# A banded-convolution stage on TensorE in larger products: up to ten tiles per product, one head per PSUM bank, two rounds per unit

## The chip, the cores and the metric

The kernel runs on one core of a Trainium2 chip. The metric is the device time of one execution in microseconds (us). Engines are named PE (TensorE, matrix products), PEld (its weight loads), DVE (VectorE), ACT (ScalarE), POOL (GpSimd, which here issues nearly all input transfers) and SP (which issues most output transfers).

A ratio below is the mean time of one kernel's fast runs over the mean of the other's fast runs of the same rounds, so it is not quite the ratio of the medians that are quoted beside it. Runs over 1.5% above the fastest of the same kernel count as slow and are left out of ratios.

## The reference

The computation has two parts. A depthwise causal convolution with seven softmax-normalized taps per head (8 heads of 24 channels) goes over x of 8 x 3264 x 192. Its output u feeds a spectral mixing: a real FFT along the sequence, the lowest 64 modes multiplied by complex 192 x 192 matrices, an inverse FFT, a residual, and a ReLU branch.

```python
out = np.einsum('hk,bskhg->bshg', w, x_unf)          # seven taps, per head
X = np.fft.rfft(x, axis=1)                           # x is the convolution's output
Yr = einsum('bmd,mde->bme', Xr, w_r) - einsum('bmd,mde->bme', Xi, w_i)
Yi = einsum('bmd,mde->bme', Xr, w_i) + einsum('bmd,mde->bme', Xi, w_r)
y = np.fft.irfft(Y, n=S, axis=1)
u = x + y
return u + np.maximum(u @ w_ch, 0.0)
```

## The kernel before

x lies in SBUF as bf16 tiles of 128 sequence positions: 26 tiles for each of four pairs of batches (104 slots in all).

**The convolution.** Taps are put into 64 x 64 band matrices, and PE runs four 64 x 64 array tiles side by side: lower and upper 64 rows, to lower and upper 64 output partitions. Each PSUM bank receives products from a lower and from an upper row tile. A turn (an empty instruction that waits for the earlier products) separates the two steps, so that another row tile follows on a bank only when the first is done. A unit is 4 or 5 tiles of all eight heads: 32 products, two steps each of 8 per half. ACT and DVE each copy half of the heads out of PSUM.

```python
UNITS = ((0, 5), (5, 5), (10, 4), (14, 4), (18, 4), (22, 4))      # per pair of batches
...
def conv(q, t0, n):
    done = [conv_step(q, t0, n, half, 0) for half in range(2)]
    for half in range(2):
        turn(done[half])
        conv_step(q, t0, n, half, 1)
    ...                                   # half 0 copied out by ScalarE, half 1 by VectorE
```

**What is laid between the convolution's units.** The angle tables (parts 2 and 3 are built after the first two units), the low-frequency transform (`dft_unit`, into a `low` bank), and transposes of finished tiles (`some`, one bank of eight blocks per call).

```python
for k, u in enumerate(units):
    conv(*u)
    if k < 2:
        table(*PARTS[k + 1])
    ...
    if k:
        q, t0, n = units[k - 1]
        dft_unit(q, t0, n)
        ...
            some(XJOBS[k], min(NT * q + t0 + n, NT * (NQ - 1)))
```

**The weights of the mixing.** They come in 16 groups of 0.59 MB (as bf16). There are buffers for eight groups: four in `arena`, four lent by `cc`, the not yet needed transposed x of the last pair. Loads of groups 8 to 11 wait for mixing groups 0 to 3; loads of 12 to 15 wait for groups 8 to 11.

```python
for g in range(NL + NW):                  # NL = 4, NW = 4
    load_w(g)

def mix(g):
    ...                                   # 12 products with wbuf(g)
    if g < NW:
        load_w(g + NW + NL)
    elif g >= NW + NL:
        load_w(g + NW)
```

## Time and profile before

| kernel before | value |
|---|---|
| median of three runs | 181.06 us (180.78 to 181.16) |
| span of the profiled run | 179.3 us |
| input transfers without a pause | about 5 to 105 us |
| convolution on PE (L303) | 10.5 to 71.2 us, 816 products |
| mixing group 0 starts | 74.31 us |
| mixing group 15 starts | 106.82 us |
| output stage | 72.5 us |

Read it in two stages. Up to group 15 the transfers of x (at about 190 GB/s written) and then of the weights (at about 206) fill the time; after it PE fills the output stage. The GB/s row of the page's slices shows a pause in the transfers as a lower number, and the time at which group 0 starts tells how late PE is.

### The profile page before, as it was taken

To read this page: it belongs to the slowest core of one execution; us is meant where nothing else is said; L and a number is where in the kernel's file an instruction comes from. 1 tells how busy PE (TensorE), PEld (TensorE's weight loads), DVE (VectorE), ACT (ScalarE), POOL (GpSimd) and SP (SyncE) were. 2 spreads that over 40 slices of the span, in tenths; PEclk is the share of its full clock that TensorE was granted. 3 is DMA by queue.
4 is the path that set the end of the run, shared out by engine and by line. 5 is a ranking of instruction groups with operands and counts; after the bars stand their busy time and mean duration, and the time that the engine had idled before them with its cause. 6 is when DMAs were issued, how large, how long until landed. Compare 5 with 4: busy or idle time off the path is not lost.

```text
span 179.3 us, 6296 instructions
## 1 busy us (share of the span) xinstructions
PE 147.0 (82%) x2736; PEld 109.0 (61%) x2736; DVE 112.1 (63%) x159; ACT 98.4 (55%) x134; POOL 68.8 (38%) x113
## 2 busy tenths in 40 slices
PE   0047569999999999699677769999999999999940
PEld 0034337666667666477465757888776778888820
DVE  1878555674865675334435443788676878888870
ACT  8176643735553734247445355576775676666630
POOL 7999998878866534335244000000000500000000
PEclk9999979999999999979999999999999999999995
DMA  3999999999999999999999950589987799999993
GB/s 42 170 181 188 190 189 189 190 192 190 192 191 190 205 207 206 206 206 206 206 206 206 207 93 4 173 275 300 366 296 268 227 324 362 364 358 347 356 362 131
DMA packets 62875, 40.17 MB, mean 224 GB/s; under 512 B 28800, under 2 KB 62784, under 8 KB 62848
## 3 DMA queue, kind: packets, MB, share of 16 engines
q0 software_dynamic: 36224, 20.08, 80.5%
q1 hardware_dynamic: 26624, 19.69, 32.7%
q8 instruction: 21, 0.34, 0.8%
q14 instruction: 6, 0.05, 0.1%
HBM read 39.40 MB, written 20.05 MB: 332 GB/s over the span
## 4 chain that ended last, share of the span: by engine, by line
DMA 33%; PE 29%; issue 23%; POOL 7%; DVE 4%; ACT 1%; DVEq 0%; POOLq 0%
DMA arena<-in_moe_w_i_dram 13%; PE z L303 8%; DMA cc<-in_moe_w_i_dram 6%; PE low L329 6%; DMA arena<-in_moe_w_r_dram 5%; DMA out_dram<-arena 5%; POOL xall L145 4%; DMA xall<-in_x_dram 3%; PE za L508 3%; PE zb L508 3%; PE za L488 3%; PE zb L488 2%; PE low L383 2%; DVE xall L323 1%; DVE arena L559 1%
## 5 line engine op out<-in xcount | busy, mean ns | idle before, releaser
L303 PE MATMUL z<-xall,band 64*64 64x192 bf16 (+3 forms) x816 | 27.4, 263 | 16.3 <-ACT band L189 10.5
L145 POOL DMA_DIRECT2D xall<-in_x_dram x48 | 38.5, 814 | 5.2 <-DMA xall<-in_x_dram 2.7
L323 DVE CAST xall<-z 128x768 bf16<-128x768 f32 (+1 forms) x24 | 24.5, 1021 | 14.4 <-PE z L303 13.7
L303 PEld LDWEIGHTS <-band 64*64 64x64 bf16 x816 | 18.3, 110 | 24.5 <-ACT band L189 10.9
L321 ACT CAST xall<-z 128x768 bf16<-128x768 f32 (+1 forms) x24 | 20.4, 850 | 22.1 <-PE z L303 22.1
L488 PEld LDWEIGHTS <-cc 64*128 64x128 bf16 x600 | 27.1, 94 | 6.6 <-issue 1.8
L559 DVE TENSOR_TENSOR arena<-za,xall 128x768 f32<-128x768 f32 x26 | 24.8, 956 | 6.1 <-ACT za L534 2.0
L534 ACT ACTIVATE za<-za 128x768 f32<-128x768 f32 (+1 forms) x27 | 21.0, 783 | 9.5 <-PE za L508 9.2
L559 DVE TENSOR_TENSOR arena<-zb,xall 128x768 f32<-128x768 f32 x23 | 21.9, 956 | 6.3 <-ACT zb L534 2.9
L534 ACT ACTIVATE zb<-zb 128x768 f32<-128x768 f32 (+1 forms) x25 | 19.6, 782 | 10.1 <-PE zb L508 8.6
L329 PE MATMUL low<-xall,ftab 128*128 128x384 bf16 x100 | 21.6, 343 | 0.0
L383 PEld LDWEIGHTS <-xall 128*128 128x128 bf16 x300 | 18.7, 105 | 3.2 <-issue 0.3
L548 POOL DMA_DIRECT2D out_dram<-arena x4 | 2.4, 615 | 42.4 <-DVE arena L540 42.4
L488 PE MATMUL za<-wc,cc 64*128 64x192 bf16 x318 | 17.9, 243 | 0.4 <-DVE arena L559 0.4
L508 PE MATMUL za<-mixa,ftab 64*128 64x384 bf16 (+1 forms) x120 | 18.1, 304 | 0.0
L508 PE MATMUL za<-mixa,fsin 64*128 64x384 bf16 (+1 forms) x120 | 18.1, 304 | 0.0
L358 DVE COPY cc<-r 128x1024 bf16<-128x1024 bf16 (+1 forms) x16 | 10.2, 670 | 12.3 <-ACT xs L444 6.0
L508 PE MATMUL zb<-mixa,ftab 64*128 64x384 bf16 (+1 forms) x100 | 16.1, 313 | 0.4 <-ACT zb L534 0.4
L508 PE MATMUL zb<-mixa,fsin 64*128 64x384 bf16 (+1 forms) x100 | 16.1, 313 | 0.0
L488 PE MATMUL zb<-wc,cc 64*128 64x192 bf16 x282 | 15.9, 243 | 0.0
L356 ACT COPY cc<-r 128x1024 bf16<-128x1024 bf16 (+1 forms) x9 | 8.9, 990 | 10.2 <-PE r L383 8.2
L508 PEld LDWEIGHTS <-ftab 64*128 64x128 bf16 x220 | 11.8, 94 | 3.9 <-issue 1.5
(108 smaller groups left out, 185.2 us busy)
## 6 DMA issues: line engine op xcount, KB each, us to landing
out_dram<-arena SPq DMA_DIRECT2D x45, 384.0 KB, 4.6
xall<-in_x_dram POOLq DMA_DIRECT2D x24, 192.0 KB, 6.9
xall<-in_x_dram POOLq DMA_DIRECT2D x16, 240.0 KB, 6.7
arena<-in_moe_w_r_dram POOLq DMA_DIRECT2D x12, 288.0 KB, 9.5
arena<-in_moe_w_i_dram POOLq DMA_DIRECT2D x12, 288.0 KB, 10.1
out_dram<-arena SPq DMA_DIRECT2D x10, 192.0 KB, 2.5
xall<-in_x_dram POOLq DMA_DIRECT2D x8, 144.0 KB, 6.3
cc<-in_moe_w_r_dram POOLq DMA_DIRECT2D x4, 288.0 KB, 11.8
```

Source lines behind the costliest of these rows:

```text
L145: nc.gpsimd.dma_start(out=xall[:, s0:s0 + nf, i, :], in_=src)
L303: mm = nc.tensor.matmul(ov[c], band[r, h, c.start + shift + 64 * (r is UP and c is LO): c.start + shift + 64 * (r is UP and c is LO) + 64] ...
L321: nc.scalar.copy(out=dst, in_=srcv)
L323: nc.vector.tensor_copy(out=dst, in_=srcv)
L329: nc.tensor.matmul(xp, ftab[:, t, :], xall[:, slot(q, t), :, :], start=(t == 0), stop=False, skip_group_check=True)
L356: nc.scalar.copy(out=out, in_=in_)
L358: nc.vector.tensor_copy(out=out, in_=in_)
L383: nc.tensor.transpose(tp[:, P * k:P * k + P], src, ident[:])
L488: nc.tensor.matmul(zt[:, i, D * k:D * k + D], cc[r, q, 3 * t + j, :], wc[r, j, :], start=(k == 0 and j == 0), stop=False, skip_group_check ...
L508: nc.tensor.matmul(zt[:, i, D * k:D * (k + w)], tabs[c][r, t, :], zw[r, q:q + w, c, which, :], start=False, stop=end and k + w == len(duo) ...
L534: nc.scalar.activation(out=zt[:, :, 0:w], in_=zt[:, :, 0:w], func=ACT.Relu)
L559: nc.vector.tensor_tensor(out=o[:, :, :].rearrange("p k (i d) -> p i k d", i=2), in0=zt[:, :, 0:2 * D].rearrange("p i (k d) -> p i k d", k=2),
```

## The change

The intent is fewer and longer products. A unit is up to ten tiles and is done in two rounds of four heads; one head fills one bank, so a product has up to 480 columns instead of 240. The last two units stay at four tiles. Convolution products fall from 816 to 496.

```diff
+    cunits = [(q, t0, n) for q in range(NQ) for t0, n in (((0, 5), (5, 5), (10, 8), (18, 8)) if q == 0 else
+                                                         ((0, 10), (10, 8), (18, 8)) if q < NQ - 1 else
+                                                         ((0, 10), (10, 8), (18, 4), (22, 4)))]
...
-    def conv_step(q, t0, n, half, step):
+    def conv_step(q, t0, n, hp, step):
...
-                o = cp[:, jj, 0:2 * GRP * n].rearrange("p (t i e) -> p t i e", t=n, i=2)
+            o = Z[hp % 2][:, j, 0:2 * GRP * n].rearrange("p (t i e) -> p t i e", t=n, i=2)
...
-    def conv(q, t0, n):
-        done = [conv_step(q, t0, n, half, 0) for half in range(2)]
-        for half in range(2):
-            turn(done[half])
-            conv_step(q, t0, n, half, 1)
+    def conv(q, t0, n, part):
+
+        hps = (2 * part, 2 * part + 1)
+        done = [conv_step(q, t0, n, hp, 0) for hp in hps]
+        for hp, names in zip(hps, done):
+            turn(names)
+            conv_step(q, t0, n, hp, 1)
...
-    for k, u in enumerate(units):
-        conv(*u)
-        if k < 2:
-            table(*PARTS[k + 1])
...
+    for k, u in enumerate(cunits):
+        for part in range(2):
+            conv(*u, part)
+            if part and k < 2:
+                table(*PARTS[k + 1])
...
+                n0 = (n + 1) // 2
+                dft_unit(q, t0 + n0 * part, n - n0 if part else n0)
...
+                    some(part or k % 3 == 0, min(NT * q + t0 + n, NT * (NQ - 1)))
```

More of the change, by code (lines that the diff above doesn't have):

```diff
@@ L266 @@
     LO, UP = slice(0, 64), slice(64, P)
-    def conv_step(q, t0, n, half, step):
-        cp = Z[half][:, :, :].rearrange("p k (j c) -> p (k j) c", j=2)
+    def conv_step(q, t0, n, hp, step):
         s0 = slot(q, t0)
@@ L274, in conv_step @@
         last = t0 + n == NT
-        end = step == 1
         res = []
-        for j in range(2):
-            for own in (True, False):
-                jj = 2 * ((step if own else 1 - step)) + j
-                h = 4 * half + jj
-                dsl = slice(GRP * h, GRP * h + GRP)
-                o = cp[:, jj, 0:2 * GRP * n].rearrange("p (t i e) -> p t i e", t=n, i=2)
-                first = step == 0 and j == 0
-                cur, prev = xall[:, s0 + 1:s0 + 1 + n, :, dsl], xall[:, s0 + k0:s0 + n, :, dsl]
-                if own:
-                    ms = [(LO, LO, o, cur, 0), (UP, UP, o, cur, 0)]
-                    if last:
-                        ms.append((UP, UP, o[:, n - 1, 0, :], xall[:, s0 + n - 1, 1 - q // 2, dsl], 64))
-                else:
-                    m, k1 = (n - 1 if last else n), (n - 1 if last and q >= 2 else n)
-                    ms = [(LO, UP, o[:, 0:m, :, :], cur[:, 0:m, :, :], 0),
-                          (UP, LO, o[:, k0:k1, :, :], prev[:, 0:k1 - k0, :, :], 64)]
-                    if k1 < n:
-                        ms.append((UP, LO, o[:, n - 1, 0, :], xall[:, s0 + n - 1, 1, dsl], 64))
-                res.append([(r, c, ov, mv, h, shift, first) for r, c, ov, mv, shift in ms])
@@ L297, in conv_step @@
-        names = []
-        for pair in (res[0:2], res[2:4]):
-            for k in range(3):
-                for lst in pair:
-                    if k < len(lst):
-                        r, c, ov, mv, h, shift, first = lst[k]
-                        mm = nc.tensor.matmul(ov[c], band[r, h, c.start + shift + 64 * (r is UP and c is LO):
-                                                          c.start + shift + 64 * (r is UP and c is LO) + 64],
-                                              mv[r], start=first and k < 2, stop=end, skip_group_check=True,
-                                              tile_position=(r.start, c.start))
-                        names.append(mm.ins.name)
@@ L308, in conv_step @@
-        return names[-6:]
-    def conv(q, t0, n):
-        done = [conv_step(q, t0, n, half, 0) for half in range(2)]
-        for half in range(2):
-            turn(done[half])
-            conv_step(q, t0, n, half, 1)
-        s0 = slot(q, t0)
-        for half in range(2):
-            cp = Z[half][:, :, :].rearrange("p k (j c) -> p (k j) c", j=2)
-            dst = xall[:, s0:s0 + n, :, 96 * half:96 * half + 96].rearrange("p t i (j e) -> p j (t i) e", j=4)
-            srcv = cp[:, :, 0:2 * GRP * n].rearrange("p j (c e) -> p j c e", e=GRP)
-            if half == 0:
+        for own in (True, False):
+            j = step if own else 1 - step
+            h = 2 * hp + j
+            dsl = slice(GRP * h, GRP * h + GRP)
+            o = Z[hp % 2][:, j, 0:2 * GRP * n].rearrange("p (t i e) -> p t i e", t=n, i=2)
+            cur, prev = xall[:, s0 + 1:s0 + 1 + n, :, dsl], xall[:, s0 + k0:s0 + n, :, dsl]
+            if own:
+                ms = [(LO, LO, o, cur, 0), (UP, UP, o, cur, 0)]
+                if last:
+                    ms.append((UP, UP, o[:, n - 1, 0, :], xall[:, s0 + n - 1, 1 - q // 2, dsl], 64))
+            else:
+                m, k1 = (n - 1 if last else n), (n - 1 if last and q >= 2 else n)
+                ms = [(LO, UP, o[:, 0:m, :, :], cur[:, 0:m, :, :], 0),
+                      (UP, LO, o[:, k0:k1, :, :], prev[:, 0:k1 - k0, :, :], 64)]
+                if k1 < n:
+                    ms.append((UP, LO, o[:, n - 1, 0, :], xall[:, s0 + n - 1, 1, dsl], 64))
+            res.append([(r, c, ov, mv, h, shift) for r, c, ov, mv, shift in ms])
@@ new lines, in conv_step @@
+        names = []
+        for k in range(3):
+            for lst in res:
+                if k < len(lst):
+                    r, c, ov, mv, h, shift = lst[k]
+                    b0 = c.start + shift + 64 * (r is UP and c is LO)
+                    mm = nc.tensor.matmul(ov[c], band[r, h, b0:b0 + 64], mv[r], start=step == 0 and k < 2,
+                                          stop=step == 1, skip_group_check=True, tile_position=(r.start, c.start))
+                    names.append(mm.ins.name)
@@ new lines, in conv_step @@
+        return names
+    def conv(q, t0, n, part):
[4 more added lines that the diff above has]
+            conv_step(q, t0, n, hp, 1)
+        s0 = slot(q, t0)
+        for hp in hps:
+            dst = xall[:, s0:s0 + n, :, 2 * GRP * hp:2 * GRP * hp + 2 * GRP].rearrange("p t i (j e) -> p j (t i) e", j=2)
+            srcv = Z[hp % 2][:, :, 0:2 * GRP * n].rearrange("p j (c e) -> p j c e", e=GRP)
+            if hp % 2 == 0:
@@ L399, in some @@
                 f(*a)
-    XJOBS = [k % 3 != 1 for k in range(len(units))]
     waiting = []
-    for k, u in enumerate(units):
-        conv(*u)
-        if k < 2:
-            table(*PARTS[k + 1])
-        if waiting:
-            xtrans(*waiting.pop(0), 0)
-        if k:
-            q, t0, n = units[k - 1]
-            dft_unit(q, t0, n)
-            if t0 + n == NT:
-                waiting = [(q, 0), (q, 1)]
-            if k > 1:
-                some(XJOBS[k], min(NT * q + t0 + n, NT * (NQ - 1)))
-    dft_unit(*units[-1])
+    for k, u in enumerate(cunits):
[3 more added lines that the diff above has]
+                table(*PARTS[k + 1])
+            if waiting:
+                xtrans(*waiting.pop(0), 0)
+            if k:
+                q, t0, n = cunits[k - 1]
+                n0 = (n + 1) // 2
+                dft_unit(q, t0 + n0 * part, n - n0 if part else n0)
+                if part and t0 + n == NT:
+                    waiting = [(q, 0), (q, 1)]
+                if k > 1:
+                    some(part or k % 3 == 0, min(NT * q + t0 + n, NT * (NQ - 1)))
+    dft_unit(*cunits[-1])
     NG = MODES // 4
```

## The prediction

> **What bounds the kernel now.** I read the page first: the slices, then the chain, then the issues. The rows here are the page's slices.
>
> ```profile
> PE   0047569999999999699677769999999999999940
> DMA  3999999999999999999999950589987799999993
> GB/s 42 170 181 188 190 189 189 190 192 190 192 191 190 205 207 206 206 206 206 206 206 206 207 93 4 173 275 300 366 296 268 227 324 362 364 358 347 356 362 131
> ```
>
> One slice is 179.3/40 = 4.48 us. From slice 2 to slice 23 (about 5 to 105 us) the transfers never pause: near 190 GB/s for thirteen slices, then a flat 206. After one empty slice the output begins. So there are two stages: an input stage of about 106 us and an output stage of about 72 us. TensorE (PE) also reads 9 from slice 7 to slice 16, so that digit alone does not say which of the two sets the end of the input stage. Bytes do: the first rate belongs to x (8x3264x192 values written as bf16, 10.03 MB, 10.03/0.190 = 53 us) and the second to the mixing weights (2x64x192x192 in bf16, 9.44 MB, 9.44/0.2065 = 46 us). Starting near 5 us these give 104 us with no gap between them.
>
> Next I asked who waits at the place where the two streams meet: the first rows of the view of the mixing matmul (L435), then those of the timeline near the end of the input stage.
>
> ```profile
> L435 PE MATMUL low<-arena,mixa x144: 245/246/368, 74.3 to 107.0; 128*16 128x192 bf16 x144
> its engine sat idle before it (us, times) until:
>   DMA arena<-in_moe_w_i_dram: 14.2, 16
> ```
>
> ```profile
> 101.09 0.46 PE L435 MATMUL low<-arena,mixa 128*16 128x192 bf16 x12 [0.93 <-DMA arena<-in_moe_w_i_dram]
> ...
> 103.98 0.46 PE L435 MATMUL low<-arena,mixa 128*16 128x192 bf16 x12 [0.75 <-DMA arena<-in_moe_w_i_dram]
> ...
> 105.55 0.37 PE L386 MATMUL r<-ident,xall 128*64 128x128 bf16 x6
> ...
> 106.82 0.46 PE L435 MATMUL low<-arena,mixa 128*16 128x192 bf16 x12 [0.68 <-DMA arena<-in_moe_w_i_dram]
> 107.20 0.44 PEld L488 LDWEIGHTS <-cc 64*128 64x128 bf16 x12
> ```
>
> The mixing groups start 2.9 us apart (101.09, 103.98, 106.82), each after waiting for its weights. One group is 0.59 MB, and 0.59/0.2065 = 2.86 us. This is the pace of the transfers. Group 15 starts at 106.82, and 179.3 - 106.8 = 72.5 us of output stage follow. The windows say what limits that stage:
>
> ```profile
> 80.00:90.00 10.00, 8.22 (x181) 6.32 (x175) 4.69 (x10) 5.59 (x10) 3.66 (x6) 1.00 1.21 206
> 150.00:160.00 10.00, 10.00 (x180) 8.35 (x177) 8.34 (x10) 6.85 (x10) 0.00 (x0) 1.00 1.10 367
> ```
>
> Columns after the stretch: PE, weight load, VectorE (DVE), ScalarE (ACT), GpSimd, clock, DMA, GB/s. In the output stage PE has no gap and the chain of waits runs through its L488 and L508; the convolution has no part in it.
>
> Where is the convolution (L303)? PE does it from 10.5 to 71.2 us. The chain of waits goes through it from 24 to 57 us, but then leaves it for the weight transfers:
>
> ```profile
> 55.62 0.96 PE z L303 x21
> 56.58 0.02 issue
> 56.60 0.81 ACT xall L321
> 57.41 0.40 issue
> 57.81 0.61 POOL arena L424
> ```
>
> I do not believe this join. The transfer issue at L424 also waits for an earlier transfer of the same queue (the built order shows that wait on every issue), and the DMA row has no dent at 57 us. ScalarE's latest dependence there is the angle table, finished tens of microseconds before. So L303 on the chain is an inference of the view. PE arrives late at the mixing, but the weights keep flowing for other reasons.
>
> **What the Trainium skill says.** "TensorE: Matmul & The Clock Gate", on LDWEIGHTS and the isolated gap, gives N/2.4 + 2.5 ns between warm matmuls of N columns: 82.5 ns for 192, 102.5 for 240. In this trace 32 matmuls, four array tiles at a time, take 0.89 us for 192 columns (chain, x32 pieces), 0.89/8 = 111 ns per four; 240 columns take 1.01 us, 126 ns. The trace is 24 to 29 ns above the page, and that remainder per set of four is what fewer, longer products can save. "TensorEngine Tiling (Array Packing)", Restrictions and Gotchas, Gotcha 1, says that different row tiles cannot access the same PSUM bank at once and that software must synchronize; that is the turn-taking wait in both kernels, and no run yet shows its price. Its section Performance Considerations, PSUM Bottleneck, says that tiling speeds up TensorE but not the copying out of PSUM. The trace agrees that copies cost by elements: DVE 958 ns for 768 and 1158 for 960, so 1.04 ns per element plus about 158 fixed; ACT 798 and 966, so 0.875 plus about 126.
>
> **The change part by part.**
> 1. Fewer products. 816 L303 matmuls become 496: 24x32 + 48 against 14x32 + 48 (the 48 are the 24-column edge products). All data is still streamed. With the page's gap plus 25 ns, estimates for a set of four are 160 + 2.5 + 25 = 187 ns at 384 columns and 228 ns at 480. Eight tiles: 16 x 111 = 1.78 us before, 8 x 187 = 1.50 after, 0.28 saved. Ten tiles: 16 x 126 = 2.02 before, 8 x 228 = 1.82 after, 0.20 saved. Seven pairs merge to eight and three to ten: 7 x 0.28 + 3 x 0.20 = 2.6 us less PE time in the input stage. If the fixed part vanished altogether it would be about 5 us.
> 2. Two rounds per unit. Each round has four sets of four, two before and two after the turns. There are 28 copies each on ACT and DVE instead of 24, of the same total elements: 4 x 158 = 0.6 us more on DVE and 4 x 126 = 0.5 us on ACT. Both engines are about 65% and 50% busy there (30 to 70 us windows).
> 3. The low-frequency transform (L329) is spread over the rounds; its 100 matmuls stay.
> 4. Transposes: by the loop's rule there are 16 banks in this stage instead of 15, so one fewer remains after mixing group 14. That removes about 0.54 us of PE at 104 to 106 us, where PE then waits for group 15's weights anyway (0.68 us).
> 5. Transfers: number, order and waits are identical in the built order. Nothing in the output stage changes.
>
> Sum on the path: the input stage ends at its last weight, 106.8 + 0; output 72.5 + 0. The 2.6 us lie beside transfers. PE should finish the convolution near 68.5 instead of 71.2 and start group 0 near 71.5 instead of 74.3, then meet the weights' pace a few groups earlier and wait longer. Expected change of the end: 0.0 us.
>
> **The rivals.**
> A. The convolution really gates the end, as the chain suggests. Then 2.6 to 5 us less PE would give 176 to 178.5 us, 1.4 to 2.8% faster. For: PE digits of 9 and the chain. Against: 206 GB/s in every slice after x, 14.2 us of mixing matmuls waiting for weights, group spacing equal to 2.86 us. An earlier mixing group frees a buffer earlier, but an already full queue is not made faster by that.
> B. The turns cost more now: only one set of another bank lies between a set and its successor, about 187 ns, where there were two (222 ns). If each of 56 turns lost 150 ns, PE would be 8.4 us longer, minus 2.6, so group 0 near 80. The last weight transfer not gated by mixing was issued at 72.72 and landed at 83.84 (chain), so the queue would still hold work, and PE has over 1 us to regain per group early on, more than half of it unused. I would then expect 181 to 183. Only beyond about 8 us of lateness does the queue run dry.
> C. Starvation at the start: an eight-tile unit needs more x before it begins. It is 0.79 MB, 4.1 us of transfer, but PE already runs about 11 us behind the transfers near 60 us, so data are there. Against the final value this is hidden like B; the last two units stay at four tiles, so the last dependence on x is no coarser.
> D. A longer idle time of PE before mixing could lower the clock (0.83 granted at 70 to 80 us). If it spilled into the output stage it might cost some tenths of a microsecond; the groups just before that stage keep their work, so this should not happen.
>
> **Range and chances.** The three runs before lie within 0.38 us. I centre on no change, 181.0 us. Small timing shifts at the stage boundary and another chip make 180.1 to 182.0 my eight-in-ten range. Rival A gets 4% for faster by over 2% (it needs the upper half of its savings), B with C gets 2% for slower by over 2% (it needs 3.6 us exposed), and 94% stays within 2%.
>
> **What will show each step.** Right: L303 has 496 matmuls, ends near 68 us; GB/s remains near 190 and then 206 without a dent; group 15 starts at 106.8 within 0.5 us and waits longer or equally for its weights; idle time of L435 on transfers grows from 14.2 us; output stage 72.5 us. Step 1 is wrong if a 384-column set of four takes far from 187 ns; step 2 if PE waits repeatedly for ACT or DVE at L303. The prediction is wrong if the transfers finish earlier than 105 us (rival A: they were gated by PE), or if a dent appears between x and the weights or near 75 us (rival B), or if the output stage's length changes.

## The result, and the profile after

The changed kernel took 183.77 us (median of six, 182.58 to 185.33) against 181.34 (six) for the kernel before. The ratio of fast runs is 1.0119, 95% interval 1.0085 to 1.0153. It is slower by 1.2%, outside the range that I had given. The profiled run (183.82 us, fast, span 181.9 us) shows where. First the page's slices of the changed kernel; a slice is 181.9/40 = 4.55 us, and I count slices from 0 here, where the prediction counted from 1.

```profile
PE   0037437999999999969999678999999999999940
PEclk9999995799999999999999999999999999999995
DMA  4999999999999999996999990269989699999995
GB/s 50 160 181 188 190 191 189 190 190 191 192 190 192 208 206 206 206 193 89 195 206 206 206 161 1 87 223 365 356 296 317 170 331 364 369 343 365 357 331 173
```

There is a dent that was not there before: 193, 89 and 195 in slices 17 to 19 (77 to 91 us). Against 206 that is (13 + 117 + 11)/206 x 4.55 = 3.1 us of transfers not made. PE has low digits (3, 7, 4, 3, 7) in slices 2 to 6, and the clock fell there too. Then the view of the mixing matmul (engine, operation, count, ns min/median/max, first and last start):

```profile
L435 PE MATMUL low<-arena,mixa x144: 245/246/291, 82.0 to 109.9; 128*16 128x192 bf16 x144
its engine sat idle before it (us, times) until:
  DMA arena<-in_moe_w_i_dram: 8.3, 10
```

Group 0 starts at 82.0 us instead of 74.3, and PE waits for weights less (8.3 us instead of 14.2): it is the late party, not the early one. The timeline of POOL, the issuer of the weight transfers, ties both together. Changed kernel first, then the kernel before; the bracket is POOL's idle time ahead of an issue and what ended it.

```profile
71.86 0.61 POOL L424 DMA_DIRECT2D cc<-in_moe_w_i_dram  x1 [0.81 <-DMA arena<-in_moe_w_i_dram]
82.78 0.61 POOL L424 DMA_DIRECT2D arena<-in_moe_w_r_dram  x1 [10.31 <-PE low L435]
```

```profile
72.72 0.61 POOL L424 DMA_DIRECT2D cc<-in_moe_w_i_dram  x1 [1.42 <-DMA arena<-in_moe_w_i_dram]
75.09 0.61 POOL L424 DMA_DIRECT2D arena<-in_moe_w_r_dram  x1 [1.75 <-PE low L435]
```

The last load that needs no freed buffer is issued at 71.9 us. The next waits for mixing group 0 and goes out 10.9 us later. In that time the queue empties. Group 15 moves from 106.82 to 109.72 us, by 2.9 us. The output stage keeps its length: 181.9 - 109.7 = 72.2 us against 72.5.

So the question is why PE, with 320 products fewer, is 7.7 us later at group 0. The starts of the convolution in the two timelines split this:

| start of | before | after | lateness |
|---|---|---|---|
| tile 18 of the first pair | 27.59 | 31.70 | 4.1 |
| second pair | 31.61 | 36.88 | 5.3 |
| third pair | 44.80 | 50.11 | 5.3 |
| fourth pair | 57.93 | 63.39 | 5.5 |
| mixing group 0 | 74.31 | 82.00 | 7.7 |

In the steady middle a pair takes 13.2 us in both kernels: the longer products save nothing. 5.3 us are lost in the start and 2.2 in the last pair. One caution: the granted clock was near 0.5 at 24 to 28 us in this profile of the kernel before and at 27 to 34 us in that of the changed one. The runs before_late4 and before_late8 below, with the code of before up to about 69 us and without that drop, start tile 18 at 26.09 us, so against them the first four rows are about 1.5 us later still.

The start: the last table wait in the timeline of the kernel before, then of the changed one.

```profile
18.95 0.95 PE L303 MATMUL z<-xall,band 64*64 64x192 bf16 x32 [1.14 <-ACT xall L321]
...
22.04 0.99 ACT L205 ACTIVATE ftab<-arena,halfpi 128x832 bf16<-128x832 f32 x1
22.94 0.78 ACT L321 CAST xall<-z 128x768 bf16<-128x768 f32 x1
...
23.77 1.65 PE L303 MATMUL z<-xall,band 64*64 64x192 bf16 x32 [2.50 <-ACT xall L321]
```

```profile
22.35 1.43 PE L303 MATMUL z<-xall,band 64*64 64x384 bf16 x16
...
26.75 0.99 ACT L209 ACTIVATE ftab<-arena,halfpi 128x832 bf16<-128x832 f32 x1
27.64 0.78 ACT L320 CAST xall<-z 128x768 bf16<-128x768 f32 x1
...
28.48 1.69 PE L303 MATMUL z<-xall,band 64*64 64x384 bf16 x16 [4.10 <-ACT xall L320]
```

ACT works in order. The copy out of PSUM stands behind the whole table part, and PE cannot reuse the banks until the copy is done. With two rounds per unit, a round more has to pass through this jam before the next table part is even begun, and what each wait holds up is half a unit: after the last of these waits the kernel before has 14 tiles done at 23.8 us, the changed one 10 tiles and half of eight at 28.5.

### The profile page after: what moved, and what is told of

Same layout as the page of the kernel before. It is cut to its first block, busy times and chain, and to the rows that moved or that the text cites. A ratio compares the mean times of both kernels' runs of the same rounds, so it can differ in the third digit from the quotient of the medians.

```text
span 181.9 us, 5665 instructions
## 1 busy us (share of the span) xinstructions
PE 148.5 (82%) x2416; PEld 103.8 (57%) x2416; DVE 113.6 (62%) x163; ACT 98.4 (54%) x138; POOL 68.9 (38%) x113
## 4 chain that ended last, share of the span: by engine, by line
PE 36%; DMA 12%; DVE 2%; issue 1%; POOL 1%; DVEq 0%
DMA arena<-in_moe_w_i_dram 12%; PE za L508 9%; PE zb L508 8%; PE za L488 8%; PE zb L488 6%; DVE arena L559 1%; PE low L435 1%; PE r L371 1%; POOL arena L424 1%; PE zb L515 1%; DVE arena L554 1%; PE low L515 1%; PE za L515 0%; PE zb L500 0%; PE zb L481 0%
## 5 line engine op out<-in xcount | busy, mean ns | idle before, releaser
L303 PE MATMUL z<-xall,band 64*64 64x384 bf16 (+6 forms) x496 | 30.2, 341 | 20.6 <-ACT band L193 10.5
L322 DVE CAST xall<-z 128x768 bf16<-128x768 f32 (+3 forms) x28 | 25.2, 899 | 21.5 <-PE z L303 20.5
L320 ACT CAST xall<-z 128x768 bf16<-128x768 f32 (+3 forms) x28 | 21.1, 752 | 25.2 <-PE z L303 21.1
L303 PEld LDWEIGHTS <-band 64*64 64x64 bf16 x496 | 14.2, 110 | 35.6 <-issue 15.4
L328 PE MATMUL low<-xall,ftab 128*128 128x384 bf16 x100 | 22.3, 345 | 0.0
L357 DVE COPY cc<-r 128x1024 bf16<-128x1024 bf16 (+1 forms) x16 | 10.8, 675 | 8.4 <-PE r L382 6.2
L424 POOL DMA_DIRECT2D arena<-in_moe_w_r_dram x12 | 7.5, 622 | 19.4 <-PE low L435 17.7
```

Source lines behind the costliest of these rows:

```text
L303: mm = nc.tensor.matmul(ov[c], band[r, h, b0:b0 + 64], mv[r], start=step == 0 and k < 2, stop=step == 1, skip_group_check=True, tile_posit ...
L320: nc.scalar.copy(out=dst, in_=srcv)
L322: nc.vector.tensor_copy(out=dst, in_=srcv)
L328: nc.tensor.matmul(xp, ftab[:, t, :], xall[:, slot(q, t), :, :], start=(t == 0), stop=False, skip_group_check=True)
L357: nc.vector.tensor_copy(out=out, in_=in_)
L424: nc.gpsimd.dma_start(out=wbuf(g)[64 * half:64 * half + 64, :, :, :], in_=src[4 * g:4 * g + 4, :, :].rearrange("m (p j) e -> p m j e", j=3))
```

## The experiments

Sixteen further kernels ran. Two theories are combined: **Q**, lateness of PE at mixing group 0 costs nothing until the weight queue runs dry, and then it costs; and **S**, most lateness is made in the start, by table work ahead of the copies. The rivals are named with each run. "G0" and "G15" are the starts of mixing groups 0 and 15 in the profiled run.

| run | G0 | G15 | median us | ratio to before, interval |
|---|---|---|---|---|
| before | 74.3 | 106.8 | 181.3 | 1 |
| changed | 82.0 | 109.7 | 183.8 | 1.0119 (1.0085 to 1.0153) |
| before_late4 | 76.4 | 108.7 | 182.5 | 1.0036 (0.9988 to 1.0083) |
| before_late8 | 80.4 | 108.4 | 183.6 | 1.0129 (1.0097 to 1.0162) |
| after_oldstart | 75.8 | 107.1 | 181.2 | 0.9999 (0.9954 to 1.0043) |
| after_noturn (wrong results) | 79.8 | 107.8 | 183.2 | 1.0068 (1.0017 to 1.0118) |
| after_notables | 73.4 | 107.1 | 182.2 | 1.0033 (0.9953 to 1.0113) |
| after_oldend | 80.9 | 108.8 | 183.9 | 1.0124 (1.0092 to 1.0157) |
| after_fewjobs | 78.6 | 109.5 | 184.1 | 1.0120 (1.0055 to 1.0185) |
| before_noturn (wrong results) | 72.6 | 107.3 | 181.5 | one run |
| after_nl6 | 81.3 | 106.7 | 181.8 | 1.0007 (0.9970 to 1.0044) |
| after_spread | 73.9 | 107.8 | 183.3 | 1.0077 (1.0039 to 1.0114) |
| before_notables | 70.5 | 107.3 | 181.1 | one run |
| spread_nl6 | 73.8 | 107.8 | 181.5 | 1.0021 (0.9977 to 1.0064) |
| spread_warm | 73.5 | 107.5 | 181.7 | 0.9993 (0.9952 to 1.0035) |
| spread_jobs15 | 73.7 | 107.5 | 181.8 | 0.9965 (0.9908 to 1.0022) |
| before_warm | 75.1 | 107.4 | 181.6 | 0.9993 (0.9953 to 1.0034) |
| spread_nl6_warm | 73.6 | 107.9 | 182.1 | 1.0014 (0.9971 to 1.0058) |

### Making the kernel before late

```diff
+    for r in range(48):                    # 24 in before_late4
+        nc.tensor.matmul(low[1][:, 0:2 * D], ftab[:, r % NF, :], xall[:, slot(0, r % NF), :, :], start=True, stop=True,
+                         skip_group_check=True)
     dft_unit(*units[-1])
```

> The kernel before with 24 extra 384-column matmuls (about 0.16 us each in the chain, 3.9 us) ahead of its last low-frequency transform, written to a bank that nobody reads before it is overwritten. Theory Q (lateness of PE at mixing group 0 costs nothing until the queue of weight transfers runs dry, and then nearly one for one; dry from a start of group 0 near 79 us): group 0 at about 78.2 us instead of 74.3, no dent in GB/s, 181.0 to 181.8 us. Rival R (PE really is on the path all along, any lateness comes out at the end): 185 us.

> The same with 48 extra matmuls, 7.8 us. Theory Q: group 0 at about 82.1 us as in the changed kernel, a dent of about 3 us in GB/s between 76 and 85 us, 183.5 to 184.5 us, so the changed kernel's time without its convolution. Rival R: 189 us. Rival H (the slack is over 8 us as I had predicted, and the changed kernel lost its time elsewhere): 181.3 us.

With 24 products, group 0 came at 76.4 us (the clock had not dropped at the start of this run, so the run was earlier than expected). There is no dent near 80 us and the ratio is 1.0036 with an interval that holds 1, though the median of 182.5 us lies above the 181.0 to 181.8 expected. The profiled run's G15 of 108.7 comes from elsewhere: its GB/s row is already low in slices 2 to 6 (169, 177, 159, 186, 182), before any added product. With 48 products group 0 came at 80.4 us, the GB/s row shows a dent of 175 and 202, and the ratio is 1.0129, just what the changed kernel has, with the convolution of before. The windows of 2 us (columns after the stretch: PE, PEld, DVE, ACT, POOL, clock, DMA share, GB/s) place the dent:

```profile
80.00:82.00 2.00, 1.61 (x50) 1.25 (x52) 0.87 (x2) 0.08 (x1) 0.83 (x2) 1.00 1.16 197
82.00:84.00 2.00, 2.00 (x62) 1.54 (x56) 1.22 (x4) 1.48 (x3) 1.75 (x4) 1.00 1.00 145
84.00:86.00 2.00, 2.00 (x62) 1.58 (x56) 0.99 (x3) 1.35 (x3) 2.00 (x4) 1.00 1.20 201
```

The size of the dent missed: about 0.8 us and not 3, while G15 is 1.6 us later than before. About 0.5 us of that lie in slices 2 to 4 (175, 184, 181 GB/s against 181, 188, 190), ahead of the added products, and the output stage is 0.5 us longer (181.4 - 108.4 = 73.0 us). Rival R (one for one from the start) would have given 185 and 189 us, and rival H (slack over 8 us) 181.3. Both fall. Added lateness alone makes a loss of the same size; the dent accounts for only part of it, and the rest is not explained.

### The old convolution in the first pair, and in the last two units

```diff
-    cunits = [(q, t0, n) for q in range(NQ) for t0, n in (((0, 5), (5, 5), (10, 8), (18, 8)) if q == 0 else
+    cunits = [(q, t0, n) for q in range(NQ) for t0, n in (UNITS if q == 0 else
...
+        old = isold(u)        # u[0] == 0; in after_oldend: u[0] == NQ - 1 and u[1] >= 18
+        for part in ((1,) if old else (0, 1)):
+            if old:
+                conv_old(*u)
+            else:
+                conv(*u, part)
```

> The changed kernel with the convolution of before for the first batch pair (six units, one round each) and the changed one for the other three pairs; again 16 transpose banks ahead of mixing. Theory S (most of the lateness, about 5 of 7.7 us, is made in the start, where the angle tables stand ahead of the copies out of PSUM on ScalarE and two rounds per unit wait for them with half the products done): group 0 at about 77 us, no dent, 181.0 to 181.8 us. Rival T (the turns cost in every unit): group 0 still after 80 us, dent, over 183 us.

> The changed kernel with only the last two four-tile units in the convolution of before (one round of 32 products each); the start and the rest are changed. Theory S: the lateness of the start stays, only the two units lose 2 x (2 x 0.65 - 0.89) = 0.8 us and some waits: group 0 near 80 us, ratio 1.006 to 1.012. Rival E (the end of the stage is where it went): group 0 near 77 us, ratio under 1.004.

With the old start, group 0 is at 75.8 us, the dent is gone and the ratio is 0.9999. So three quarters of the tiles in the changed convolution cost nothing at the end. With the old end, group 0 is at 80.9 us, the dent stays (198 and 147 GB/s) and the ratio stays at 1.0124. Rival E, that it went in the end of the stage, falls; the two units account for 1.1 us of lateness. The ratio is not the dent's alone: in this profile PE waited 1.63 us for group 15, the granted clock was 0.50 at 110 to 112 us, and the output stage took 182.3 - 108.8 = 73.5 us.

### Without turns

Each bank half keeps its row tile in both steps, so no turn is needed. The results are wrong on purpose.

```diff
-            j = step if own else 1 - step
+            j = 0 if own else 1
...
-            turn(names)
             conv_step(q, t0, n, hp, 1)
```

> Wrong results on purpose: each half of a PSUM bank is written by the same row tile in both steps, so that no row tile follows another on a bank, and the turn-taking wait is not needed and left out; the streamed columns are the same or a few more. Theory S alone: rounds stay near 0.9 us in the steady part, the distance between the starts of two batch pairs stays 13.2 us, group 0 after 80 us. Theory T (turns eat what the longer products save): a round of 384 columns falls from 0.88 us to about 0.70, the distance of pairs to about 12 us, group 0 near 78 us, and the dent mostly goes: 181 to 182 us.

> Wrong results on purpose: the kernel before without its turn-taking waits, as the changed one was run (each half of a bank keeps its row tile). One look at the rounds: 32 products of 192 columns took 0.89 us with two turns. If a turn is as dear as in the changed kernel (0.19 us per round of 192 columns, 0.11 of 384): about 0.70 us. If the two sets of four between hid it: 0.85 to 0.89 us.

These two runs take a round apart. The times are from one round's start to the start of what follows it, in the steady part of the timelines; a set is four products side by side, one for each 64 x 64 array tile, and the streaming column is sets x columns at 2.4 columns per ns.

| round | streaming | without turns | with turns |
|---|---|---|---|
| before, 8 sets of 192 | 0.64 | 0.78 | 0.89 |
| before, 8 sets of 240 | 0.80 | 0.94 | 1.01 |
| after, 4 sets of 384 | 0.64 | 0.77 | 0.88 |
| after, 4 sets of 480 | 0.80 | 0.94 | 1.00 |
| after, 4 sets of 192 (last two units) | 0.32 | 0.45 | 0.64 |

Between 192 and 240 columns the slope without turns is (0.94 - 0.78)/(8 x 48) = 0.417 ns per column, which is 1/2.4: the Trainium skill, "TensorE: Matmul & The Clock Gate", Back-to-back issue gap, gives N/2.4 + 2.5 ns for warm products, and the trace agrees with the slope. What is left is 0.13 to 0.14 us per round whatever the number of products, and 0.06 to 0.19 us for its two turns. The fixed price belongs to a round and not to a product. The change halves products per round and makes 28 rounds out of 24. There was nothing to save. Theory T had expected 0.70 us for a round of 384 and 12 us for a pair; 0.77 and 12.8 came out. Without turns group 0 came at 79.8 instead of 82.0 us, and the ratio of 1.0068 is between the two; here too the clock was 0.50 at 108 to 110 us, after a wait of 1.18 us for group 15. In the kernel before two turns cost 0.11 us per round, the same as for 384 columns; the two sets between did not hide them. Its group 0 came at 72.6 instead of 74.3 us, but most of that is the clock at the start, which did not drop in this run: it ended its transposes ahead of the last transform at 69.44 us, and before_late8, also without the drop, at 69.66. With shorter rounds PE paused elsewhere (0.20 and 0.41 us near 53 and 59 us, no releaser shown).

### Without the later tables

Parts 2 and 3 of the tables are left out; ACT writes zeros instead, in idle time before the first product. The result was still within the tolerance, presumably because the mixing weights are small, but it is not the reference's function.

```diff
+    nc.scalar.activation(out=ftab[:, PARTS[1][0]:, :]..., in_=halfpi[:].to_broadcast(...), func=ACT.Copy, scale=0.0)
...
             if part and k < 2:
-                table(*PARTS[k + 1])
+                pass
```

> Wrong results on purpose: the changed kernel without the second and third part of the angle tables; those entries are zeros, written by ScalarE while it waits for the first product's weights. The first part stays. Theory S (the table work ahead of the copies makes 4.7 us of the 7.7 us of lateness): the unit of tile 18 of the first pair starts before 26 us instead of 31.7, group 0 near 76 to 77 us, no dent, ratio to before 1.000 to 1.004. Rival C (the start is late because an eight-tile unit waits for its transfers): the start moves by less than 1 us, group 0 after 80 us, ratio near 1.012.

> The kernel before without the second and third part of the tables (zeros; results may pass or fail). One look: what the tables cost the one-round form. If they cost both forms the same, tile 18 starts near 20 us (27.6 less 7.8); if two rounds make them dearer, as theory S says, the kernel before gains 3 to 5 us, so near 23 to 24 us. The time stays near 181 us in either case, because group 0 is only earlier.

In the changed kernel tile 18 of the first pair starts at 23.94 us instead of 31.70, so 7.8 us earlier; in the kernel before at 23.44 instead of 27.59, 4.2 us earlier. Both forms then start tile 18 within 0.5 us of each other. The tables cost the two-round form 3.6 us more than the one-round form, and that is nearly all of the 4.1 us of lateness at this point. (Both profiles with tables carry about 1.4 us of the lower clock here: from the last wait to tile 18 the changed kernel takes 3.2 us, 1.8 without tables, and the kernel before 3.8 us, 2.4 in before_late8. It hardly changes the difference. How much of the lower clock is itself due to PE's waits for the tables was not tested.) Rival C, waiting for the eight-tile transfers, falls. The dent is gone. The ratio, 1.0033, has a wide interval: two of three fast runs took 180.9 and 181.1 us, one 183.2 at a lower clock. That scatter comes up again below.

### Fewer transposes ahead of mixing

```diff
-                    some(part or k % 3 == 0, min(NT * q + t0 + n, NT * (NQ - 1)))
+                    some(part and k % 2 == 0, min(NT * q + t0 + n, NT * (NQ - 1)))
...
-    PLAN = (1, 2, 1, 2, 1, 2, 1, 2, 3, 3, 3, 3, 3, 3, 99)
+    PLAN = (2, 2, 2, 2, 2, 2, 2, 3, 4, 4, 4, 4, 4, 4, 99)
```

> The changed kernel untouched in its convolution, with 6 transpose banks ahead of mixing instead of 16; the 10 others follow between mixing groups, where PE waits for weights. 10 x 0.54 = 5.4 us less ahead of mixing. Theory Q: group 0 near 76.6 us, no dent, group 15 near 107 us, ratio 1.000 to 1.004, with the changed convolution as slow as ever. If the convolution's rounds themselves cost the end: ratio stays near 1.012. If the moved banks only push the end out elsewhere: PE busy before group 15 and over 1.01 without a dent.

This one missed. Group 0 came only 3.4 us earlier, not 5.4, and no better time came out (1.0120). PEld's idle time ahead of L303 with no releaser shown rose from 15.4 to 19.1 us: the transposes had covered such waits between rounds. And with four banks after each group from 8 on, mixing ran at 2.3 to 2.65 us per group from 91.4 us, and the loads of groups 12 to 15 are gated by groups 8 to 11: the GB/s row has a dent of 156, 187, 197 in slices 20 to 22 instead. The profiled run was a slow one, so I take only the kind of it: the gate has a second opening, and moved work was late there.

### Two more weight buffers, convolution untouched

Transposed x of the last but one pair lends space too, so ten groups are loaded before a mixing group must free a buffer.

```diff
-    late = cc[:, NQ - 1, :, :].rearrange("p k s -> p (k s)")
-    NL = CB * P // WGB
+    NL = 6
+    late = cc[:, NQ - 2:NQ, :, :].rearrange("p q k s -> p (q k s)")[:, 2 * CB * P - NL * WGB:]
+    LIM = NT * (NQ - 2) + 16
...
-                    some(part or k % 3 == 0, min(NT * q + t0 + n, NT * (NQ - 1)))
+                    some(part or k % 3 == 0, min(NT * q + t0 + n, LIM))
...
-        some(PLAN[g], NT * (NQ - 1) if g < NW + NL - 1 else NT * NQ)
+        some(PLAN[g], LIM if g < NW + NL - 1 else NT * NQ)
```

> The changed kernel, convolution untouched, with two more weight buffers lent by the transposed x of the last but one pair (ten groups, not eight, are loaded before a mixing group must free a buffer; the transposes into that region wait for mixing group 9). Theory Q: group 0 as late as before, near 82 us, but the queue stays full until about 79 + 2 x 2.86 = 84.7 us, so no dent, group 15 near 107 us, ratio to the kernel before 0.998 to 1.004. Rival (the changed convolution costs the end by another way, such as slower transfers beside its copies or a clock that drops later): the dent or the longer output stage stays, ratio 1.008 to 1.015.

Theory Q passes its sharpest test. Windows of 2 us again, first the changed kernel, then this one:

```profile
80.00:82.00 2.00, 0.54 (x12) 0.39 (x12) 1.02 (x2) 0.46 (x1) 0.00 (x0) 1.00 1.00 167
82.00:84.00 2.00, 2.00 (x64) 1.65 (x66) 0.69 (x1) 0.47 (x1) 1.22 (x3) 1.00 0.14 22
84.00:86.00 2.00, 2.00 (x58) 1.45 (x54) 1.12 (x3) 1.31 (x4) 1.77 (x4) 1.00 0.94 126
```

```profile
80.00:82.00 2.00, 1.05 (x34) 0.76 (x32) 1.02 (x2) 0.00 (x0) 0.00 (x0) 1.00 1.22 207
82.00:84.00 2.00, 2.00 (x61) 1.58 (x56) 0.91 (x2) 1.10 (x2) 1.83 (x3) 1.00 1.21 206
84.00:86.00 2.00, 2.00 (x62) 1.56 (x60) 0.90 (x3) 1.35 (x4) 0.94 (x2) 1.00 1.20 205
```

PE is as late as ever (group 0 at 81.3 us), the transfers never pause, group 15 starts at 106.7 us and the ratio is 1.0007. So no other cost of the changed convolution shows beyond the noise of these runs (0.9970 to 1.0044).

### The same table work, spread

```diff
-            if part and k < 2:
-                table(*PARTS[k + 1])
+            for p, i in SPREAD.get((k, part), ()):
+                steps[p][i]()          # one of a part's six instructions at a time, from round (0, 0) to round (3, 0)
```

> The changed kernel with the same table work cut into its six instructions and laid between the rounds, so that ScalarE never holds a copy out of PSUM behind a whole part of the tables. Theory S: the unit of tile 18 of the first pair starts near 26 us instead of 31.7, group 0 near 77 us, no dent, ratio 0.998 to 1.005. If it is the amount of table work and not its place: start and group 0 stay within 1 us of the changed kernel's, ratio 1.01.

Theory S holds for the lateness, better than I had expected: tile 18 starts at 23.9 us and group 0 at 73.9 us with all tables built, and there is no dent. Yet the ratio was 1.0077. The windows at the border of the two stages show a second loss:

```profile
106.00:108.00 2.00, 0.19 (x8) 0.19 (x12) 0.00 (x0) 0.48 (x2) 0.00 (x0) 0.70 0.07 12
108.00:110.00 2.00, 1.90 (x26) 0.99 (x18) 0.17 (x1) 0.38 (x2) 0.00 (x0) 0.50 0.00 0
110.00:112.00 2.00, 1.92 (x14) 1.19 (x16) 0.77 (x3) 0.42 (x2) 0.00 (x0) 0.50 0.00 0
```

PE waited 2.07 us for the weights of group 15, the clock fell to half, and the output stage began with it: 12 products L511 took 1.14 us there instead of 0.67. The span ends 182.6 - 107.8 = 74.8 us after group 15, not 72.5. (That run itself counts as slow, 184.3 us; the fast ones took 181.6 to 183.9.) The run with both mends, tables spread and ten groups, fell into two clumps: four runs at 181.1 to 181.7 us and two at 183.1 and 183.2.

> Both mends in the changed kernel: tables spread, two more weight buffers. Theory Q and S: no dent, PE early, and the end still set by the transfers and the output stage: ratio 0.995 to 1.002, no faster than the kernel before by over 0.5%, with less scatter between runs than the changed kernel's 182.6 to 185.3. If PE time ahead of mixing had been on the path: faster by 1% or more.

### Keeping PE warm while it waits for weights

```diff
             mix_trans(g // 2)
+        if g >= 8:
+            for r in range(12):
+                nc.tensor.matmul(low[(g // 2 + 1) % 2][:, 2 * D:2 * D + P], ident[:], xall[:, slot(0, r), 0, 0:P],
+                                 start=True, stop=True, skip_group_check=True)
```

In spread_jobs15 nothing is added; one transpose bank is moved back behind mixing group 14 by letting `some` do one fewer ahead (`and k < 12`).

> The changed kernel with the tables spread (group 0 at 73.9 us, no dent, yet ratio 1.0077) and 12 dummy 128-column matmuls (about 0.8 us) after each of mixing groups 8 to 14, where PE waits for weights; written to columns that nobody reads. Theory W (the rest is the clock: PE idle 2.07 us ahead of group 15, granted clock 0.50 from 108 to 112 us, so the output stage starts at half speed and loses about 2 us): clock 1.00 after 106 us, ratio 0.997 to 1.003. Rival S2 (the rest is a loss in the output stage that has nothing to do with idle time): ratio stays 1.005 to 1.010.

> The changed kernel with the tables spread, but one transpose bank fewer ahead of mixing (15 as in the kernel before, not 16), so that three banks and not two lie between mixing groups 14 and 15. Theory W: the idle time ahead of group 15 falls by about 0.5 us and the clock drops in fewer of the runs: ratio 1.000 to 1.005, below the 1.0077 of the spread kernel. Rival S2: unchanged, 1.0077 within its interval.

> The kernel before with the same dummy matmuls. Control: they cost the kernel before nothing to 0.3 us, as PE waits for weights there (0.68 to 0.93 us per group). If the clock also drops at the border of stages in some of its own runs, it gains: ratio 0.995 to 1.001. If the dummies delay mixing by themselves: above 1.002.

> The version to which the runs point: changed convolution, tables spread, two more weight buffers, PE kept warm. Theory Q, S and W: group 0 near 74 us, no dent, clock 1.00 at the border, 180.3 to 181.5 us, ratio 0.994 to 1.001, and less scatter than spread with two buffers alone (181.1 to 183.2). If PE ahead of mixing mattered beyond the queue: faster by 1% or more.

With the dummies the spread kernel went from 1.0077 to 0.9993, and all six runs lie within 180.97 to 182.15 us. (The two ratios are from different rounds, on different chips; the spread kernel without dummies was not run again beside it.) Its windows keep the clock:

```profile
106.00:108.00 2.00, 1.54 (x34) 1.16 (x32) 0.58 (x2) 0.91 (x2) 0.00 (x0) 1.00 0.06 10
108.00:110.00 2.00, 1.77 (x26) 1.22 (x28) 0.41 (x2) 0.53 (x2) 0.00 (x0) 1.00 0.00 0
```

This fits theory W against rival S2, a loss without idle time. spread_jobs15 has 0.9965, below what was expected, with fast runs of 180.1 to 182.1 us, but two of its six runs (183.0 and 183.8) were slow, so I do not read it as a gain. In its profile PE waited 0.78 us for group 15 and the clock was 1.00; the drop may still have happened in the two slow runs, which are not profiled. That this run lost nothing without dummies, on the chip of spread_warm, weakens the case for the dummies. before_warm costs and gains nothing (0.9993), with less scatter (180.9 to 181.9 against 180.8 to 183.1). All mends together gave 1.0014. No version beat the kernel before clear of noise; it was already at the pace of its transfers.

The clock of the unprofiled runs is known only as a mean, so that each 183 us run of these kernels had the drop at the border is argued from the profiles and from spread_warm, not shown run by run. The wait alone does not decide it: 1.18, 1.63 and 2.07 us ahead of group 15 (after_noturn, after_oldend, after_spread) were followed by 0.50, 1.10 us in the changed kernel and 1.12 us in after_nl6 by 1.00.

## Why the prediction was wrong

In short: I had PE start group 0 near 71.5 us and the queue full up to about 8 us of lateness. PE started at 82.0 us, mostly because the second round per unit met the tables in the start, and the queue ran dry from about 5 us of lateness.

**What bounds the kernel.** Right for the kernel before: transfers, then PE. after_notables and spread_warm bring group 0 to about 73.4 us, before_notables to 70.5, and none is faster. The join on the chain that I did not believe was indeed not on the path. Rival A falls.

**Step 1, fewer products: wrong.** I took 25 ns per set of four as a price of each set, and expected 187 ns at 384 columns and 2.6 us saved. The round of four sets took 0.88 us, 220 ns per set. What a set of 192 columns took above streaming (0.25 us of a round over eight sets, 31 ns) did not belong to the set: 0.14 us are per round and 0.11 us are its turns. With four sets per round each set carries twice that. Two rounds took 1.78 us before and 1.76 after, so 0.02 saved instead of 0.28 per eight tiles.

**Step 2, two rounds: the failed step.** I counted the 0.6 us more of copies and saw both engines at 50 to 65% in the middle. I did not look at the start, where ACT holds copies behind tables and a second round per unit passes through it. This is 3.6 us by the two runs without tables. The profiled run also had a lower clock from about 27 to 34 us (the clock row reads 5 and 7 in slices 6 and 7), and its round at 31.70 us took 1.60 us instead of 0.93. At the last pair, rounds of four sets of 192 columns took 0.64 to 0.70 us, so two of them cost more than one old round of 0.89.

**Rival B: right in kind, wrong in size.** I named a queue that runs dry, and put its edge at 8 us of lateness, because the last ungated transfer had landed at 83.84 us. It is about 5 us: no dent at this place with group 0 at 76.4 and 78.6 us, small ones at 79.8 and 80.4 (about 0.9 and 0.8 us), the full one at 82.0. The queue has to be refilled before it is empty. The changed kernel issues again at 82.78 us, and the windows show 167 GB/s for 80 to 82 us, 22 for 82 to 84 and 126 for 84 to 86. So the rate falls before the last transfer has landed, and 126 of 206 is as if the full flow began at 84.8 us, about 2 us after the issue (an estimate from these windows); both should have come off the slack. The Trainium skill, "DMA: Bandwidth & Descriptors", Anatomy of one DMA, gives a fixed 2.0 us for such a transfer, but it puts most of that after the last byte, so it is not this delay. I also gave the turns as the reason for lateness, at 150 ns for each of 56. Without them group 0 came 2.2 us earlier, 39 ns for each. In the kernel before they cost PE's end only about 0.2 us, once the clock at the start is the same (69.44 against 69.66 us). So the turns may explain up to 2 of the 7.7 us; the profiles differ in clock, and this share is not shown more closely.

**Rival D: a real effect, in other versions of the changed kernel.** I had said the clock should not drop into the output stage. In after_spread it did, with an output stage longer by 2.3 us, and in after_noturn and after_oldend as well. In the changed kernel's own profile the clock was 1.00 there.

**Step 4 and step 5.** One bank was moved as I said, but the wait ahead of group 15 grew (0.68 to 1.10 us), not far from the 1.18 us after which after_noturn had the lower clock; "nothing" was too quick. The output stage was as forecast, 72.2 us; the transfers were not, with 3.1 us of pause.

## What to carry to other kernels

Work that is hidden behind transfers is hidden only as long as it frees buffers in time: find when the last transfer that needs no freed buffer ends, take off the time to refill the queue, and what is left is the slack. Before merging products, find out whether the overhead belongs to the product or to the round (its turns, its copies); a change that halved the products of a round and kept about as many rounds saved nothing here. An in-order engine that also builds tables turns each additional hand-over in the start into a wait, so lay such work in small pieces.

## What the Trainium skill lacked or had wrong

- "TensorEngine Tiling (Array Packing)", Gotcha 1, states that row tiles must be synchronized on a bank, but not what it costs: two turns took 0.06 to 0.19 us per round here (0.64 against 0.45 us for 16 products of 192 columns), and a round had 0.13 to 0.14 us more above streaming.
- "TensorE: Matmul & The Clock Gate", Why this matters for your kernels, warns of idle gaps over about 3 us. Keeping below that was not enough here: an idle wait of 2.07 us, with little work before it, was followed by a granted clock of 0.50 from 108 to 112 us, and waits of 1.63 and 1.18 us in two other runs were followed by 0.50 as well.
- No page gives how early a transfer queue has to be refilled to stay full. With eight transfers of 0.29 MB outstanding, lateness beyond about 5 us showed (no dent with group 0 at 78.6 us, a first one at 79.8), although the last transfer landed over 9 us after group 0's usual start in the kernel before (83.84 against 74.31 us).
